# Splitting the first FFN weight behind its decode, with a power of two per row, mostly on GpSimd

## The chip, the core and the metric

The kernel runs on one NeuronCore of a Trainium2 chip. The core has five engines with instruction queues of their own, each of which runs its instructions in order: TensorE (PE in the profile; its weight loads are PEld), VectorE (DVE), ScalarE (ACT), GpSimd (POOL) and SyncE (SP, which here only issues DMAs). The metric is the device time of one execution in microseconds. The kernel before took 1120.02 us in the median of three runs (1115.86 to 1120.48).

## The reference

Causal attention with a forget-gate-like bias, followed by a two-layer FFN without an expert choice. Batch 8, 8 heads, 576 positions, head size 64; so x has 4608 rows of 512, the hidden layer has 2048. The two FFN weights arrive as float64.

```python
scores = scale * q @ k.T                      # scale = 1/8
cum = cumsum(maximum(s, 0))
scores = where(causal, -1e9, scores + minimum(-(cum_q - cum_k), 0))
attn = softmax(scores)
x = (attn @ v) as rows of 512                 # 8 heads side by side
h = x @ w_in                                  # 512 x 2048
g = where(h >= 1, h, where(h <= -1, 0, (h + 1)**2 / 4))
y = g @ w_out                                 # 2048 x 512
```

## The kernel before

**Products in two halves.** The FFN's products run in float16, but each operand is held as a high and a low half (`hi = f16(w * r)`, `lo = f16(w * r - hi)`), and three of the four half products are summed in PSUM. `r` is a power of two that brings the operand into float16's range. For the first weight (`w1`, `w_in`) there is one `r` for the whole weight before the change; for the second (`w2`, `w_out`) one for each half of its columns.

**The first weight.** `w_in` comes in 16 chunks of 128 x 512 numbers of 8 bytes (512 KB each): chunk c holds row block c // 4 of the weight (the 128 rows that are multiplied with head pair c // 4 of x) and column block c % 4. `Weights.load` issues a chunk's DMA; four raw buffers go round. `Weights.decode` turns a chunk from float64 into float32 in place in `WO[c]`: |w| on ACT (L203), the running peak (L204) and a shift (L205) on DVE, then for even chunks a byte shuffle on ACT (L210) and one DVE instruction (L211), for odd chunks two DVE instructions (L213, L214). When all 16 are decoded, `Weights.scale` forms the maximum over all peaks: a DVE reduction (L219), a transpose on PE (`row_wi`, L110), a few DVE instructions on one number, and a product with ones on PE that spreads it over the partitions (`col_wi`, L120). Then `Weights.split` writes the halves into `WI[c]`: hi on ACT (L232); lo on DVE in one instruction (L240) for eleven chunks, and for the five chunks of `POOL_LO` on GpSimd in two, a scaling in place (L235) and a subtraction (L238). The second weight goes the same way; its raw chunks use three buffers, and its first three loads are ordered behind the scale of the first weight (L190 copies that bound into the raw tile).

**Attention.** A job (n, hf) is a head pair n and a part hf of the query rows (hf 0: rows 0 to 319 in three tiles, hf 1: rows 320 to 575 in two). For each tile and head: scores on PE into PSUM (`s`, L409 for the first 12 jobs in plain float32, L412/L413 later), DVE adds the mask and finds the minimum (L418), ACT takes the exponential (L429). The first four jobs (`plain`, head pairs 0 to 3, hf 0) are done in float32: GpSimd scales the weights by the reciprocal sums (L446), PE transposes them into PSUM (`pp`, L450), ACT copies them (`pt`, L451), and PE multiplies with v (`px`, L502). Later jobs are split in halves and transposed by DMA (`pb`, `pt`, L476 to L483; `px`, L510). In all jobs px is then split into the two halves of x (L520 on ACT, L521 on DVE); the float32 jobs scale it by `exs`, a number of the batch.

**FFN.** For each batch b, part hf and block of 128 hidden columns (16 of them): `ffn_h` multiplies x with `WI` (12 matmuls, L562), ACT and DVE form the activation (L574, L577, L578), ACT and GpSimd split it (L588, L589), and `ffn_y` multiplies with `WO` (L601) into four PSUM banks `y0` to `y3`.

**Order.** The kernel is written as a list of steps: first the four float32 jobs with the decode of one first-weight chunk in every second slot, then the scale and the split of the first weight, then a loop in which attention slots, the decode and split of the second weight, and the FFN alternate. A scheduler with priorities then fixes every engine's order before the run; each engine follows its list in order, so an instruction whose input is late holds everything behind it on that engine.

The pieces of work that the change and the prediction touch are printed here.

Of the kernel before, what the change touches and what calls it, by code (L numbers as in the profile page):

```python
# [57 lines left out]
ACT_LOW = {'wi': range(0, 16, 2), 'wo': range(0, 16, 2)}  # L58
POOL_LO = {'wi': (2, 3, 7, 11, 15), 'wo': range(1, 16, 2)}
POOL_SCALE = ('wi',)  # L60
# [16 lines left out]
def attention_ffn(ctx: ExitStack, tc: tile.TileContext, qT, kT, vn, s, w_in, w_out, yT):  # L77
# [97 lines left out]
    class Weights:  # L175
        def __init__(self, name, src, held, out, tags, groups):
            self.size = NW // groups
# [3 lines left out]
            self.r = [cp.tile([P, 1], F32, name=f"r_{name}{g}") for g in range(groups)]  # L181
            self.raw = {}
            self.act_low, self.pool_lo = ACT_LOW[name], POOL_LO[name]

# [12 lines left out]
        def decode(self, c):  # L197
# [14 lines left out]
            else:  # L212
                V.scalar_tensor_tensor(wi, hw, -0x40000000, wi, ALU.bitwise_and, ALU.bitwise_or)  # L213
                V.scalar_tensor_tensor(wi, lw, 29, wi, ALU.logical_shift_right, ALU.bitwise_or)  # L214

        def scale(self, g, least):
            bound, r = self.bound[g], self.r[g]
            t = cp.tile([P, 1], F32, name=f"t_{self.name}{g}")
            V.tensor_reduce(t, self.peak[:, g * self.size:(g + 1) * self.size], axis=AX, op=ALU.max)  # L219
            top = column_max(t, f"{self.name}{g}")  # L220
            b = top.bitcast(I32)
            V.tensor_scalar(b, b, 3, -0x40000000, ALU.logical_shift_left, ALU.bitwise_xor)
            V.tensor_scalar(b, b, 0x7FFFFFFF, None, ALU.bitwise_and)
            pow2floor(top, top, least)
            spread(bound, top, f"{self.name}{g}")
            V.reciprocal(r, bound)
            V.tensor_scalar(r, r, 2.0 ** 14, None, ALU.mult)

        def split(self, c):
# [13 lines left out]
        "wi", lambda c: w_in[c // 4 * P:(c // 4 + 1) * P, c % 4 * NC:(c % 4 + 1) * NC, :],  # L243
        WO, WI, ((gp, "g", G_BUFS),), 1,
    )
# [17 lines left out]
    def batch_start(b):  # L263
        c = ap.tile([P, NPAIR], F32, tag="csc", name=f"c{b}")
        for p in range(NPAIR):
            v = vraw[b, p].rearrange("p j n -> p (j n)")
            V.tensor_reduce(c[:, p:p + 1], v, axis=AX, op=ALU.max, apply_absolute_value=True)  # L267
        t = ap.tile([P, 1], F32, tag="mt", name=f"mt{b}")
        V.tensor_reduce(t, c, axis=AX, op=ALU.max)
        top = column_max(t, f"m{b}")  # L270
        pow2floor(top, top, TINY)
        m = msc[b] = ap.tile([P, 1], F32, tag="mb", name=f"mb{b}")
        spread(m, top, f"m{b}")
        e = exs[b] = ap.tile([P, 1], F32, tag="ex", name=f"ex{b}")
        V.reciprocal(e, m)
        r = rcs[b] = ap.tile([P, 1], F32, tag="rcs", name=f"rc{b}")
        V.tensor_scalar(r, e, 4096.0, None, ALU.mult)

# [156 lines left out]
    def plain_t(n, i):  # L435
# [9 lines left out]
        for hd, Pt in enumerate(pbs.pop((n, i))):  # L445
            G.tensor_scalar(Pt[:R, :W], Pt[:R, :W], rs[:R, hd:hd + 1], 1.0, ALU.mult, ALU.mult)  # L446
            pp = ps_y.tile([P, 512], F32, tag=f"y{turn[0] % 4}", name=f"pp{n}_{i}_{hd}")
            turn[0] += 1
            for j in range(i + 1):
# [4 lines left out]
            )  # L454

    turn = [0]

# [32 lines left out]
    def att_out(n, hf):  # L490
# [3 lines left out]
        nj = tiles[-1] + 1  # L494
        PT, e = pts_.pop((n, hf)), 2.0 ** -12
        px = ps_s.tile([P, 512], F32, tag="s", name=f"px{n}_{hf}")
        if plain(n, hf):
            e = exs[b]
            for j in range(nj):
                lo = max(0, j * P - h_off)  # L500
                for hd in range(2):
# [3 lines left out]
                    )  # L505
        steps = [] if plain(n, hf) else [(j, vl, pl) for j in range(nj) for vl, pl in ((0, 0), (1, 0), (0, 1))]
        for m, (j, vl, pl) in enumerate(steps):
            lo = max(0, j * P - h_off)
            for hd in range(2):
                T.matmul(  # L510
                    px[hd * D:(hd + 1) * D, lo:N],
                    vts[n][:, vl, j, hd * D:(hd + 1) * D],
                    PT[:, 4 * j + 2 * hd + pl, lo:],
                    start=(m == 0), stop=(m == len(steps) - 1),
                )
        if p == 0:
            X[b, hf] = gp.tile([P, NKT, 2, N], F16, tag=f"x{hf}", bufs=2, name=f"x{b}_{hf}")
        x = X[b, hf]
        with tc.high_priority(offset=X_LEAD):
# [205 lines left out]
```

## Time and profile before

| | |
|---|---|
| times of three runs | 1115.86, 1120.02, 1120.48 us; median 1120.02 |
| profiled execution | 1121.97 us, of which the profile's span is 1120.2 us |
| busy share of the span | PE 91%, DVE 75%, PEld 69%, ACT 64%, POOL 60% |
| mean granted TensorE clock | 0.969 |
| instructions on GpSimd of the first weight's split (L235, L238) | 5 and 5 |

The profile's page gives the busy time of each engine, a picture of the span in 40 slices, and the costliest groups of instructions. Its timeline lists the instructions of one engine in order of time, merged where equal ones follow each other: start in us, duration in us, engine, line, operation, out<-in, sizes (partitions x elements) and count; in brackets how long the engine was idle before and whose result ended that. Its table by stretches gives the busy time of each engine between two moments, the granted TensorE clock, the share of the DMA engines' time and GB/s.

### The profile page before, as it was taken

How to read it: one execution, taken by the hardware profiler on the slowest of the kernel's cores; microseconds unless marked ns; L12 is line 12 of the kernel's file. 1: busy time of each engine (PE TensorE's matmuls, PEld its weight loads, DVE VectorE, ACT ScalarE, POOL GpSimd, SP SyncE). 2: the span in 40 equal slices, each digit the busy share in tenths (PEclk: the TensorE clock that was granted, in tenths of full speed). 3: DMA queues.
4: the chain of work that ended last, by engine and by line, in shares of the span. 5: the costliest groups of instructions: out<-in, count | busy, mean ns of one | idle time of the engine just before them, and what ended most of it. 6: DMA issues, size and time to landing. Idle time of an engine off the chain costs nothing. (4 is left out here: it accounts for less than half of the span.)

```text
span 1120.2 us, 24958 instructions
## 1 busy us (share of the span) xinstructions
PE 1018.8 (91%) x8494; PEld 777.5 (69%) x8494; DVE 844.7 (75%) x2364; ACT 716.5 (64%) x1695; POOL 676.0 (60%) x1149
## 2 busy tenths in 40 slices
PE   2584699899999999899999999999999999999998
PEld 1242366588777876687678877787678877787787
DVE  6759897678777877787778877887778877887533
ACT  3655586467557774777567764777477765777432
POOL 3446166676667665676567766666567666666522
PEclk9976799699999999999999999999999999999999
DMA  8823455546636763778548663667456762676300
GB/s 236 209 80 88 163 131 108 122 90 145 141 68 158 157 150 78 143 148 158 109 96 163 143 146 67 161 138 162 86 137 143 155 139 58 134 142 146 67 25 19
DMA packets 300839, 140.33 MB, mean 125 GB/s; under 512 B 237608, under 2 KB 286632, under 8 KB 300712
## 3 DMA queue, kind: packets, MB, share of 16 engines
q1 hardware_dynamic: 291008, 128.80, 53.5%
q10 hardware_dynamic: 9704, 9.93, 3.1%
q8 instruction: 67, 1.10, 0.4%
q14 instruction: 60, 0.49, 0.1%
HBM read 71.00 MB, written 9.73 MB: 72 GB/s over the span
## 5 line engine op out<-in xcount | busy, mean ns | idle before, releaser
L562 PE MATMUL h<-x,WI 128*128 128x256 f16 (+1 forms) x3072 | 456.8, 290 | 25.5 <-DVE u L578 20.4
L601 PE MATMUL y<-g,WO 128*128 128x256 f16 (+1 forms) x3072 | 450.9, 287 | 7.0 <-POOL g L589 4.8
L562 PEld LDWEIGHTS <-WI 128*128 128x128 f16 x3072 | 290.5, 99 | 120.5 <-issue 34.2
L601 PEld LDWEIGHTS <-WO 128*128 128x128 f16 x3072 | 288.7, 98 | 91.7 <-issue 12.5
L589 POOL TENSOR_TENSOR g<-u,g 128x320 f16<-128x320 f32 (+1 forms) x256 | 219.2, 856 | 200.6 <-ACT g L588 197.7
L429 ACT ACTIVATE p<-p,mn 64x64 f32<-64x64 f32 (+4 forms) x320 | 179.3, 560 | 135.3 <-DVE mn L418 119.0
L574 ACT ACTIVATE u<-h,ub,us 128x320 f32<-128x320 f32 (+1 forms) x256 | 149.3, 583 | 113.0 <-PE h L562 94.4
L577 DVE SCALAR_TENSOR_TENSOR h<-h,ws,u 128x320 f32<-128x320 f32 (+1 forms) x256 | 132.8, 519 | 94.4 <-ACT u L574 92.8
L418 DVE CUSTOM_DVE_ANT_0 p<-s,mask 64x64 f32<-64x64 f32 (+4 forms) x320 | 134.4, 422 | 55.8 <-PE s L413 39.0
L476 POOL TENSOR_SCALAR pb<-p,rs 128x256 f16<-128x256 f32 (+4 forms) x148 | 93.0, 629 | 134.0 <-DVE rs L472 47.9
L479 POOL TENSOR_TENSOR pb<-p,pb 128x256 f16<-128x256 f32 (+4 forms) x148 | 156.3, 1058 | 8.2
L482 DVE SCALAR_TENSOR_TENSOR pb<-p,rs,pb 128x256 f16<-128x256 f32 (+4 forms) x148 | 124.3, 840 | 20.6 <-POOL pb L476 20.4
L578 DVE SCALAR_TENSOR_TENSOR u<-u,r,h 128x320 f32<-128x320 f32 (+1 forms) x256 | 130.0, 508 | 5.2
L412 PE MATMUL s<-K1s,Q1s 128*128 128x288 f32 (+4 forms) x312 | 117.2, 378 | 10.6 <-DVE mn L418 6.7
L588 ACT CAST g<-u 128x320 f16<-128x320 f32 (+1 forms) x256 | 108.0, 422 | 22.4 <-DVE u L578 21.8
L477 ACT ACTIVATE p<-p,rs 128x192 f32<-128x192 f32 (+4 forms) x148 | 83.6, 569 | 54.9 <-DVE rs L472 54.5
L413 PE MATMUL s<-K2s,Q2s 68*128 68x288 f32 (+4 forms) x312 | 95.7, 308 | 0.1
L478 POOL TENSOR_SCALAR pb<-p 128x256 f16<-128x256 f32 (+4 forms) x148 | 92.6, 627 | 5.1 <-ACT p L477 2.5
L510 PEld LDWEIGHTS <-vt 128*64 128x64 f16 x1464 | 68.1, 112 | 19.5 <-issue 13.5
L510 PE MATMUL px<-pt,vt 128*64 128x256 f16 (+3 forms) x1464 | 77.2, 257 | 1.4 <-DMA pt<-pb 1.3
L412 PEld LDWEIGHTS s<-K1s,Q1s 128*128 128x128 f32 (+1 forms) x312 | 56.6, 182 | 22.7 <-DVE mn L418 3.8
L368 DVE TENSOR_TENSOR K2s<-rk,K1s 64x1152 fp32r<-64x1152 f32 (+1 forms) x52 | 59.2, 1139 | 7.5 <-ACT K1s L365 6.7
(131 smaller groups left out, 1013.3 us busy)
## 6 DMA issues: line engine op xcount, KB each, us to landing
rk<-in_k_dram SPq DMA_DIRECT2D x56, 288.0 KB
wir<-in_moe_w_in_dram SPq DMA_DIRECT2D x16, 512.0 KB
v<-in_v_dram SPq DMA_DIRECT2D x32, 256.0 KB
wor<-in_moe_w_out_dram SPq DMA_DIRECT2D x16, 512.0 KB
rk<-in_k_dram SPq DMA_DIRECT2D x48, 160.0 KB
rq<-in_q_dram SPq DMA_DIRECT2D x48, 160.0 KB
rq<-in_q_dram SPq DMA_DIRECT2D x56, 128.0 KB
out_dram<-o ACTq DMA_DIRECT2D x32, 160.0 KB
```

The costliest lines, as they stand in the source:

```text
L412: T.matmul(sc[:R, :c1 - c0], Q1[:, hd, qo:qo + R], K1[:, hd, c0:c1], start=True, stop=False)
L418: ttr[0] = V.tensor_tensor_reduce(out=Pt[:R, c0:c1], in0=sc[:R, :c1 - c0], in1=mask[:R, mo:mo + c1 - c0], scale=-0.125, scalar=3.0e38 if m ...
L429: A.activation(Pt[:R, :W], Pt[:R, :W], AF.Exp, bias=m2[:R], scale=-1.0, accum_out=sums[n, i][:R, hd:hd + 1])
L479: G.tensor_tensor(los[1], pw, his[1], ALU.subtract)
L482: V.scalar_tensor_tensor(los[0], pv, rs[:R, :1], his[0], ALU.mult, ALU.subtract)
L510: T.matmul(px[hd * D:(hd + 1) * D, lo:N], vts[n][:, vl, j, hd * D:(hd + 1) * D], PT[:, 4 * j + 2 * hd + pl, lo:], start=(m == 0), stop=(m ...
L562: T.matmul(h[:, :N], WI[4 * kt + ft // 4][:, wl, ft % 4 * P:(ft % 4 + 1) * P], x[:, kt, xl], start=(n == 0), stop=(n == 3 * NKT - 1),)
L574: first = A.activation(u, h[:, :N], AF.Relu, bias=ubi[b], scale=usc[b]).ins
L577: V.scalar_tensor_tensor(h[:, :N], h[:, :N], wsc[b], u, ALU.mult, ALU.max)
L578: V.scalar_tensor_tensor(u, u, r, h[:, :N], ALU.min, ALU.mult)
L589: G.tensor_tensor(g[:, 1], u, g[:, 0], ALU.subtract)
L601: T.matmul(ys[b, hf, m][:, :N], WO[8 * (m // 2) + ft // 2][:, wl, c0:c0 + P], g[:, gl], start=(ft == 0 and n == 0), stop=(ft == NFT - 1 an ...
```

## The change

Every block of 128 rows of the first weight now has a power of two of its own for each row (each partition), taken as soon as the block's four chunks are decoded (`row_scale`: five small DVE instructions, no transpose and no spreading). The chunks of a block are then split while the next block is decoded: in the code split(c - 4) follows decode(c), and the last four splits stand after the loop. Eleven chunks' lo halves go to GpSimd in two instructions, five stay on DVE; before it was five and eleven.

Because the rows of the weight now carry different powers of two, x has to carry the inverse share: `row_shares` forms the maximum over all rows (it still needs the transpose and the spreading on PE) and `shares`, a number per row, which scales x when it is split. The first four jobs' px therefore can't be split before the maximum is known: they are kept in PSUM, in the four banks of y, and split by `x_split` after the scale. The transposes pp, which used those four banks in turn, move to the two banks of h.

```diff
-POOL_LO = {'wi': (2, 3, 7, 11, 15), 'wo': range(1, 16, 2)}
+POOL_LO = {'wi': (0, 1, 2, 4, 5, 6, 8, 9, 10, 12, 14), 'wo': range(1, 16, 2)}
...
+        def exponent(self, b):
+            bi = b.bitcast(I32)
+            V.tensor_scalar(bi, bi, 3, -0x40000000, ALU.logical_shift_left, ALU.bitwise_xor)
+            V.tensor_scalar(bi, bi, 0x7F800000, None, ALU.bitwise_and)
...
+        def row_scale(self, k, least):
+            n = NW // NKT
+            b, r = self.rows[:, k:k + 1], self.r[k]
+            V.tensor_reduce(b, self.peak[:, k * n:(k + 1) * n], axis=AX, op=ALU.max)
+            self.exponent(b)
+            V.tensor_scalar(b, b, least, 2.0 ** -14, ALU.max, ALU.mult)
+            V.reciprocal(r, b)
+
+        def row_shares(self):
+            bound, e = self.bound[0], self.shares
+            t = cp.tile([P, 1], F32, name=f"t_{self.name}")
+            V.tensor_reduce(t, self.rows, axis=AX, op=ALU.max)
+            spread(t, column_max(t, self.name), self.name)
+            V.reciprocal(bound, t)
+            V.tensor_scalar(e, self.rows, bound, 2.0 ** -12, ALU.mult, ALU.mult)
+            V.tensor_scalar(bound, t, 2.0 ** 14, None, ALU.mult)
...
-            pp = ps_y.tile([P, 512], F32, tag=f"y{turn[0] % 4}", name=f"pp{n}_{i}_{hd}")
-            turn[0] += 1
+            pp = ps_h.tile([P, 512], F32, tag="h", name=f"pp{n}_{i}_{hd}")
...
         if plain(n, hf):
-            e = exs[b]
+            px = ps_y.tile([P, 512], F32, tag=f"y{p}", name=f"px{n}_{hf}")
...
+            held[n, hf] = px
+            return
...
+    def x_split(n, hf, px, shares):
...
-        x = X[b, hf]
+        x, e = X[b, hf], shares[:, p:p + 1]
         with tc.high_priority(offset=X_LEAD):
             A.activation(x[:, p, 0], px[:, :N], AF.Copy, scale=e)
             V.scalar_tensor_tensor(x[:, p, 1], px[:, :N], e, x[:, p, 0], ALU.mult, ALU.subtract)
...
                 w1.decode(c)
                 w1.load(c + 3)
+                if c >= NKT:
+                    w1.split(c - NKT)
+                if c % NKT == NKT - 1:
+                    w1.row_scale(c // NKT, LEAST_A)
...
     with tc.high_priority(offset=SCALE_LEAD):
-        w1.scale(0, LEAST_A)
+        w1.row_shares()
+        shares0 = cp.tile([P, NPAIR], F32, name="shares0")
+        V.tensor_scalar(shares0, w1.shares, rcs[0], None, ALU.mult)
         batch_scales(0)
+        for c in range(NW - NKT, NW):
+            w1.split(c)
     for c in range(3):
         w2.load(c, w1.bound[0])
-    for n in range(NW):
-        c = n % 4 * 4 + n // 4
-        w1.split(c)
     att_out(*jobs[NPAIR - 1])
+    for n, hf in jobs[:NPAIR]:
+        x_split(n, hf, held.pop((n, hf)), shares0)
```

The scheduler makes new lists of the written order. Three places matter for what follows. WO_126 to WO_141 are the first weight's 16 decoded chunks and WI_110 to WI_125 their split forms; r_wi_146 to r_wi_149 are the four row blocks' factors (before there is only r_wi_146); p_t_h is tile t and head h of the attention weights of the job at hand.

First, GpSimd at the end of the decode, where the third job's last tile (p_2) is scaled. Before:

```order
L404 MEMSET p_2_1_542 128x64
L404 MEMSET p_0_0_588 64x64
L446 TENSOR_SCALAR p_2_0_535<-p_2_0_535,rs_2_549 128x320
L446 TENSOR_SCALAR p_2_1_542<-p_2_1_542,rs_2_549 128x320
L377 TENSOR_SCALAR v_1_182<-v_1_182,rc_286 128x640
```

And in the changed kernel (L258 and L261 are the old L235 and L238, L468 is L446, L400 is L378):

```order
L258 TENSOR_SCALAR WO_138<-WO_138,r_wi_149 128x512
L426 MEMSET p_2_0_573 128x64
L426 MEMSET p_2_1_580 128x64
L258 TENSOR_SCALAR WO_140<-WO_140,r_wi_149 128x512
L400 TENSOR_TENSOR vt_943<-v_1_187,vt_943 128x640
L261 TENSOR_TENSOR WI_122<-WO_138,WI_122 128x512
L261 TENSOR_TENSOR WI_124<-WO_140,WI_124 128x512
L426 MEMSET p_0_0_630 64x64
L426 MEMSET p_0_1_637 64x64
L282 MEMSET v_1_1433 64x128
L468 TENSOR_SCALAR p_2_0_573<-p_2_0_573,rs_2_587 128x320
L468 TENSOR_SCALAR p_2_1_580<-p_2_1_580,rs_2_587 128x320
```

The split of two chunks of the last row block, which needs the last decoded chunk, and a product of v now stand ahead of the scaling that the third job's transposes wait for.

Second, DVE between the first weight's scale and its first instruction on the second weight (the peak of a decoded chunk, L204, in the change L207). Before:

```order
L240 SCALAR_TENSOR_TENSOR WI_123<-WO_139,r_wi_146,WI_123 128x512
L240 SCALAR_TENSOR_TENSOR WI_116<-WO_132,r_wi_146,WI_116 128x512
L297 TENSOR_SCALAR ws_722<-us_720 128x1
L240 SCALAR_TENSOR_TENSOR WI_120<-WO_136,r_wi_146,WI_120 128x512
L302 TENSOR_SCALAR gb_726<-gb_726 128x1
L240 SCALAR_TENSOR_TENSOR WI_124<-WO_140,r_wi_146,WI_124 128x512
L418 ISA p_4_0_919,mn_4_0_288_962<-s_4_0_288_960,mask,mn_4_0_0_923 128x288
L418 ISA mn_4_0_288_962 128x1
L521 SCALAR_TENSOR_TENSOR x_0_444<-px_0_775,ex_284,x_0_444 128x320
L471 TENSOR_SCALAR rs_3_905<-sm_3_855 128x2
L472 RECIPROCAL rs_3_905<-rs_3_905 128x2
L204 TENSOR_SCALAR WO_130,peak_wo<-WO_130 128x512
```

In the changed kernel:

```order
L549 SCALAR_TENSOR_TENSOR x_0_804<-px_0_736,shares_757,x_0_804 128x320
L312 TENSOR_SCALAR r_761<-r_761 128x1
L440 ISA p_3_1_925,mn_3_1_0_929<-s_3_1_0_927,mask 128x448
L440 ISA mn_3_1_0_929 128x1
L313 TENSOR_SCALAR r_761<-r_761 128x1
L314 TENSOR_SCALAR r_761<-r_761 128x1
L317 TENSOR_SCALAR us_769<-hs_759,r_761 128x1
L321 TENSOR_SCALAR ub_773<-r_761 128x1
L323 RECIPROCAL gb_775<-r_761 128x1
L319 TENSOR_SCALAR ws_771<-us_769 128x1
L324 TENSOR_SCALAR gb_775<-gb_775 128x1
```

The eleven L240 are gone from this stretch; three splits of x and the batch's small numbers remain, and two rows on scores and two on sums stand between the last row shown and the first L207.

Third, ACT behind the scale. Before, the sixteen hi halves stand between the last transposed copy and the first chunk of the second weight; the last four of them and what follows:

```order
L232 ACTIVATE WI_113<-WO_129,r_wi_146 128x512
L232 ACTIVATE WI_117<-WO_133,r_wi_146 128x512
L520 ACTIVATE x_0_444<-px_0_775,ex_284 128x320
L232 ACTIVATE WI_121<-WO_137,r_wi_146 128x512
L232 ACTIVATE WI_125<-WO_141,r_wi_146 128x512
L429 ACTIVATE p_3_0_856,sm_3_855<-p_3_0_856,mn_3_0_0_860 128x448
L429 ACTIVATE p_3_1_896,sm_3_855<-p_3_1_896,mn_3_1_0_900 128x448
L203 ACTIVATE WO_130<-wor_735 128x512
```

In the changed kernel:

```order
L548 ACTIVATE x_0_804<-px_0_462,shares_757 128x320
L548 ACTIVATE x_0_804<-px_0_602,shares_757 128x320
L548 ACTIVATE x_0_804<-px_0_736,shares_757 128x320
L451 ACTIVATE p_3_0_885,sm_3_884<-p_3_0_885,mn_3_0_0_889 128x448
L472 COPY pt_0_644<-pp_2_0_725 128x3x128
L472 COPY pt_0_644<-pp_2_1_731 128x3x128
L451 ACTIVATE p_3_1_925,sm_3_884<-p_3_1_925,mn_3_1_0_929 128x448
L206 ACTIVATE WO_128<-wor_788 128x512
```

The hi halves are gone from here (they stand among the decode's instructions, four after each block), and three splits of x are in their place.

More of the change, by code (lines that the diff above doesn't have):

```diff
@@ L175, in attention_ffn, with __init__ @@
     class Weights:
-        def __init__(self, name, src, held, out, tags, groups):
-            self.size = NW // groups
+        def __init__(self, name, src, held, out, tags, groups, by_rows=False):
+            self.size = NW // (NKT if by_rows else groups)
             self.name, self.src, self.held, self.out, self.tags = name, src, held, out, tags
@@ L180, in __init__ @@
             self.bound = [cp.tile([P, 1], F32, name=f"bound_{name}{g}") for g in range(groups)]
-            self.r = [cp.tile([P, 1], F32, name=f"r_{name}{g}") for g in range(groups)]
+            self.r = [cp.tile([P, 1], F32, name=f"r_{name}{g}") for g in range(NW // self.size)]
+            if by_rows:
+                self.rows = cp.tile([P, NKT], F32, name=f"rows_{name}")
+                self.shares = cp.tile([P, NKT], F32, name=f"shares_{name}")
             self.raw = {}
@@ L220, in scale @@
             top = column_max(t, f"{self.name}{g}")
[L221 to L224, printed above, removed]
+            self.exponent(top)
+            V.tensor_scalar(top, top, least, None, ALU.max)
             spread(bound, top, f"{self.name}{g}")
@@ L243, in attention_ffn @@
         "wi", lambda c: w_in[c // 4 * P:(c // 4 + 1) * P, c % 4 * NC:(c % 4 + 1) * NC, :],
-        WO, WI, ((gp, "g", G_BUFS),), 1,
+        WO, WI, ((gp, "g", G_BUFS),), 1, by_rows=True,
     )
@@ L273, in batch_start @@
         spread(m, top, f"m{b}")
-        e = exs[b] = ap.tile([P, 1], F32, tag="ex", name=f"ex{b}")
-        V.reciprocal(e, m)
         r = rcs[b] = ap.tile([P, 1], F32, tag="rcs", name=f"rc{b}")
-        V.tensor_scalar(r, e, 4096.0, None, ALU.mult)
+        V.reciprocal(r, m)
+        V.tensor_scalar(r, r, 4096.0, None, ALU.mult)
     def batch_scales(b):
@@ L454, in plain_t @@
             )
-    turn = [0]
     def weights_t(n, i):
@@ L494, in att_out @@
         nj = tiles[-1] + 1
-        PT, e = pts_.pop((n, hf)), 2.0 ** -12
-        px = ps_s.tile([P, 512], F32, tag="s", name=f"px{n}_{hf}")
+        PT = pts_.pop((n, hf))
         if plain(n, hf):
-            e = exs[b]
+            px = ps_y.tile([P, 512], F32, tag=f"y{p}", name=f"px{n}_{hf}")
             for j in range(nj):
@@ L505, in att_out @@
                     )
-        steps = [] if plain(n, hf) else [(j, vl, pl) for j in range(nj) for vl, pl in ((0, 0), (1, 0), (0, 1))]
+            held[n, hf] = px
+            return
+        px = ps_s.tile([P, 512], F32, tag="s", name=f"px{n}_{hf}")
+        steps = [(j, vl, pl) for j in range(nj) for vl, pl in ((0, 0), (1, 0), (0, 1))]
         for m, (j, vl, pl) in enumerate(steps):
@@ L515, in att_out @@
                 )
+        x_split(n, hf, px, w1.shares)
+    held = {}
+    def x_split(n, hf, px, shares):
+        b, p = n // NPAIR, n % NPAIR
+        N = HALF[hf][1]
         if p == 0:
             X[b, hf] = gp.tile([P, NKT, 2, N], F16, tag=f"x{hf}", bufs=2, name=f"x{b}_{hf}")
-        x = X[b, hf]
+        x, e = X[b, hf], shares[:, p:p + 1]
         with tc.high_priority(offset=X_LEAD):
```

## The prediction

> **What bounds the kernel now.** I read the table by stretches first, since an average over the span hides the start. Its columns are the stretch and its length, then busy time and count of PE, PEld, DVE, ACT and POOL, the granted TensorE clock, the DMA share and GB/s.
>
> ```profile
> 20.00:80.00 60.00, 39.73 (x132) 21.61 (x132) 39.16 (x154) 33.27 (x90) 25.73 (x61) 0.92 0.60 152
> 80.00:140.00 60.00, 34.00 (x147) 19.26 (x147) 52.41 (x116) 36.48 (x61) 24.19 (x26) 0.68 0.44 133
> 140.00:193.00 53.00, 50.07 (x365) 34.00 (x364) 45.21 (x111) 40.37 (x79) 37.89 (x46) 1.00 0.52 117
> 193.00:221.00 28.00, 22.00 (x128) 14.55 (x127) 19.94 (x80) 12.77 (x39) 17.31 (x37) 0.63 0.62 128
> 221.00:1060.00 839.00, 815.57 (x7242) 639.96 (x7241) 653.78 (x1839) 565.17 (x1373) 549.59 (x939) 1.00 0.61 128
> ```
>
> From 221 us on PE is busy 815.57 of 839 us at full clock: PE bounds the kernel there, and what it has done earlier it doesn't do again. The change can only move the start. In 80 to 140 us PE does 34.00 us in 60 and DVE 52.41: this stretch is DVE's. In 20 to 80 no engine is full; chains of short instructions set the pace. The second thing to read is therefore DVE's timeline behind the first weight's scale.
>
> ```profile
> 82.73 1.40 DVE L240 SCALAR_TENSOR_TENSOR WI<-WO,r_wi,WI 128x512 f16<-128x512 f32 x2
> 84.12 0.74 DVE L240 SCALAR_TENSOR_TENSOR WI<-WO,r_wi,WI 128x512 f16<-128x512 f32 x1
> 86.33 1.23 DVE L240 SCALAR_TENSOR_TENSOR WI<-WO,r_wi,WI 128x512 f16<-128x512 f32 x1
> 87.55 3.77 DVE L240 SCALAR_TENSOR_TENSOR WI<-WO,r_wi,WI 128x512 f16<-128x512 f32 x3
> 91.86 3.24 DVE L240 SCALAR_TENSOR_TENSOR WI<-WO,r_wi,WI 128x512 f16<-128x512 f32 x2
> 95.08 1.11 DVE L240 SCALAR_TENSOR_TENSOR WI<-WO,r_wi,WI 128x512 f16<-128x512 f32 x1
> 96.24 1.05 DVE L240 SCALAR_TENSOR_TENSOR WI<-WO,r_wi,WI 128x512 f16<-128x512 f32 x1
> 97.65 0.54 DVE L521 SCALAR_TENSOR_TENSOR x<-px,ex,x 128x320 f16<-128x320 f32 x1
> 98.38 0.67 DVE L204 TENSOR_SCALAR_CACHE_REDUCE WO<-WO 128x512 f32<-128x512 f32 x1
> ```
>
> The eleven lo halves take 1.40 + 0.74 + 1.23 + 3.77 + 3.24 + 1.11 + 1.05 = 12.5 us of the 15.7 between 82.73 and 98.38. Behind them wait the last part of x (97.65), without which PE can't finish a hidden block, and the first DVE instruction on the second weight (98.38). PE and the DMA queue show both waits:
>
> ```profile
> 75.33 0.37 PE L110 MATMUL row_wi<-ident,t_wi 128*1 128x128 f32 x1
> 81.90 2.18 PE L502 MATMUL px<-pt,v 128*64 128x320 f32 x10
> 98.24 1.23 PE L562 MATMUL h<-x,WI 128*128 128x320 f16 x4 [4.39 <-DVE x L521]
> ...
> 79.64 1.40 SPq L195 DMA_DIRECT2D wor<-in_moe_w_out_dram  x3
> 105.64 0.37 SPq L195 DMA_DIRECT2D wor<-in_moe_w_out_dram  x1
> ...
> 109.90 0.67 ACT L203 ACTIVATE WO<-wor 128x512 f32<-128x512 f32 x1 [3.33 <-DMA wor<-in_moe_w_out_dram]
> ```
>
> The first three loads of the second weight go out at 79.64, right behind the scale. The fourth goes out at 105.64 and ends an ACT wait at 109.90, so a load takes 4.26 us; the first would be usable at 83.9 and is first touched by DVE at 98.38.
>
> **What the change takes away here.** ACT loses sixteen hi halves, which begin in a row as soon as the scale is there:
>
> ```profile
> 79.71 8.68 ACT L232 ACTIVATE WI<-WO,r_wi 128x512 f16<-128x512 f32 x14 [0.38 <-DVE r_wi L227]
> 88.30 0.50 ACT L520 ACTIVATE x<-px,ex 128x320 f16<-128x320 f32 x1
> ```
>
> That is 0.62 us each. Without them and without DVE's 12.5 us the second weight's DVE work can begin one load and one |w| after the scale's DMA: 79.64 + 4.26 + 0.67 = 84.6 us, if the scale stays where it is. That is 98.4 - 84.6 = 13.8 us earlier. If the scale and the last float32 job come later by a slip S, the gain is 13.8 - S. The x chain says nearly the same: px ends at 84.08, its splits take 0.50 and 0.54, so PE's block could go on at 85.1 + S against 98.24, a gain of 13.1 - S. The three other splits of x, which now come after the scale too, are 1.5 us of ACT and 1.6 of DVE inside the 4.26 us in which the load is under way: nothing, and 1.5 us if the loads came at once.
>
> **What it puts ahead of it.** GpSimd's rows, and those of DVE at the end of the decode:
>
> ```profile
> 54.39 1.20 POOL L446 TENSOR_SCALAR p<-p,rs 128x320 f32<-128x320 f32 x2 [0.40 <-DVE rs L444]
> 60.74 2.25 POOL L446 TENSOR_SCALAR p<-p,rs 64x64 f32<-64x64 f32 x4 [3.08 <-DVE rs L444]
> 64.89 1.04 POOL L446 TENSOR_SCALAR p<-p,rs 128x320 f32<-128x320 f32 x2 [1.30 <-DVE rs L444]
> 67.54 1.40 POOL L378 TENSOR_TENSOR vt<-v,vt 128x640 f16<-128x640 f32 x1
> 87.37 0.75 POOL L235 TENSOR_SCALAR WO<-WO,r_wi 128x512 f32<-128x512 f32 x1
> 88.20 1.47 POOL L238 TENSOR_TENSOR WI<-WO,WI 128x512 f16<-128x512 f32 x1
> 89.65 2.22 POOL L235 TENSOR_SCALAR WO<-WO,r_wi 128x512 f32<-128x512 f32 x2
> 91.84 2.71 POOL L238 TENSOR_TENSOR WI<-WO,WI 128x512 f16<-128x512 f32 x2
> ...
> 52.44 1.68 DVE L214 SCALAR_TENSOR_TENSOR WO<-wir,WO 128x512 int32<-128x512 int32 x1
> 59.73 0.15 DVE L219 TENSOR_REDUCE t_wi<-peak_wi 128x1 f32<-128x16 f32 x1
> 61.19 0.72 DVE L214 SCALAR_TENSOR_TENSOR WO<-wir,WO 128x512 int32<-128x512 int32 x1
> ```
>
> A scaling of a chunk costs 0.75 to 1.11 us, a subtraction 1.36 to 1.47: 2.1 to 2.6 a chunk, 23 to 28 us for eleven, where GpSimd is busy 25.73 us of 60 now. By the sum they fit. By the order they don't quite. The third job's last tile is scaled at 64.89; in the new list two chunks of the last row block and a product of v stand ahead of it. They need the last decoded chunk (61.19 + 0.72 = 61.9), five small DVE instructions of 0.15 (62.7) and ACT's first hi half (63.3). Then GpSimd has 2 x 0.75 to 1.11, 1.40, and 2 x 1.36 to 1.47 to do: 5.6 to 6.5 us, so the tile is scaled at 68.9 to 69.8, 4.0 to 4.9 us late. PE's transposes of that job, its px and row_wi behind it, all in PE's order, are late by as much, and with them the scale.
>
> What of the third block's three chunks (6.3 to 7.7 us) comes on top? Their last chunk is decoded at 54.1 (the L214 of 52.44), so they can start at 55.5 and have 7.8 us, in which GpSimd also has the four scalings of 60.74 (2.25) and up to 1.2 us of the two of 54.39: 9.8 to 11.2 us of work, 2.0 to 3.4 too much. So S lies between 4.0 (all of the third block hidden) and 12.6 (4.9 + 7.7, none hidden). I take 4.5 + 3 = 7.5. Gain at the entry of the DVE stretch: 13.8 - 7.5 = 6.3 us, with bounds 1.2 and 9.8.
>
> Nothing else is on that path, as I read it. ACT's sixteen hi halves (9.9 us) go where it is busy 33.27 us of 60; DVE's five lo halves (3.5 at 0.70) and twenty small instructions (3.0) go where it is busy 39.16. Their cover is idle time between links of chains; without it the 16 us would push the decode, which the upper bound of S already allows for. The transposes' two banks in place of four make a pair wait at most for one copy of 0.5 us; px in the banks of y is gone by 95, long before y starts.
>
> **What reaches the end.** Two later places can swallow the gain.
>
> ```profile
> 109.78 18.79 SPq L195 DMA_DIRECT2D wor<-in_moe_w_out_dram  x7
> 134.30 0.18 PE L120 MATMUL col_wo<-t_wo,ones 1*128 1x1 bf16 x1 [4.62 <-DVE t_wo L118]
> 209.14 2.77 PE L510 MATMUL px<-pt,vt 128*64 128x256 f16 x30 [1.26 <-DMA pt<-pb]
> ```
>
> From 109.78 the second weight's loads go out one by one as raw buffers come free, and PE waits 4.62 us at 134.30 for a small number that stands behind them in DVE's list: this part follows the loads' pace more than its start. And in 193 to 221 PE has 22.00 us of work in 28 because attention is late (it waits for a transposed tile at 209.14): an FFN that arrives earlier waits longer for the same tile, unless attention comes earlier too. Bounds: all of the 6.3 or none. No row is nearer to one end, so I take half: 3.1 us. Against the profiled execution that is 1121.97 - 3.1 = 1118.9; this execution is 1.95 us above the median of the runs, so 1117 on the median's scale.
>
> **Rivals.**
>
> *GpSimd hides nearly all of it.* S is at its lower bound of 4.0 and the whole 9.8 us reaches the end, since DVE, which bounds 80 to 140, has 12.5 us less to do: 1120 - 9.8 = 1110. For it: GpSimd's 34 idle us. Against it: the order at 64.89.
>
> *GpSimd's queue becomes the path.* All of the attention weights of the first four jobs pass through GpSimd, in order, behind the split. If the added 23 to 28 us lie on the chain, S exceeds 13.8 and the sign turns; from S = 19.4 on it is slower by more than can be told from no change (0.5%, 5.6 us). At S = 22 it is 8 us: 1128; at 28, 1134. Against it: the jobs' chains also wait for PE, DVE and ACT.
>
> *The two engines get in each other's way.* These rows show one DVE instruction alone and a pair beside GpSimd's subtractions:
>
> ```profile
> 59.81 0.41 DVE L205 TENSOR_SCALAR WO<-WO 128x512 int32<-128x512 int32 x1
> 99.58 2.45 DVE L205 TENSOR_SCALAR WO<-WO 128x512 int32<-128x512 int32 x2
> 99.29 2.45 POOL L238 TENSOR_TENSOR WI<-WO,WI 128x512 f16<-128x512 f32 x2
> ```
>
> The pair takes 2.45 us, not 0.82, and L240 went from 0.70 to 1.26 and 1.62 in the same company. A decoded chunk has about 1.4 us of such DVE instructions (0.41, and 0.7 once or twice), twelve of them from 20 to 62 us: 17 of 42 us. Of 25 us added to GpSimd some 10 meet one; at half speed that is 5 us of DVE time on the decode. S becomes 12.5 and the gain 1.3: 1119, no change. The Trainium skill states this as a rule (GPSIMD Engine Reference, Key points: GpSimd shares its SBUF interfaces with VectorE, and contends with VectorE instructions in a two-port mode or with two SBUF inputs); the rows just shown agree with it, and it speaks against moving this work under the decode, where the kernel has most such instructions.
>
> **How the numbers follow.** Forecast (a gain of 0 to 5.5 us, middle 3): 0.40. First rival: 0.33. Queue on the path: 0.14. Contention: 0.13. Faster by over 0.5% is the first rival, 0.33; slower is the second, 0.14; within 0.5% are forecast and contention, 0.53. The range reaches from 1109, a microsecond below the first rival, to 1125, which leaves most of the second out; the forecast's own is 1114.5 to 1120.
>
> **What would show it.** Right: GpSimd's scaling of the third job's last tile, now at 64.89, between 69 and 77 us; row_wi, now at 75.33, some 7 us later; the second weight's first peak on DVE, now at 98.38, at 92 to 93; no L240 row behind the scale; the first y, which follows 134.30, 2 to 4 us earlier. Wrong: a first peak of the second weight behind 98, or row_wi behind 89, or a table by stretches in which 80 to 140 us gains but 221 us on is no shorter in sum with what lies before. Then the slip or the contention was mis-sized. A different pace from 221 us on would be outside this argument: the lists there are new too, and I have taken their pace as equal.

## The result, and the profile after

The changed kernel takes 1108.42 us in the median of four runs (1108.05 to 1110.02), the kernel before 1120.25 in the median of four beside it (1115.86 to 1121.04). The ratio is 0.9905, with a 95% interval of 0.9878 to 0.9933: faster, by 11.8 us as the medians have it and by 10.6 as the ratio has it (7.5 to 13.7). The median is 0.6 us below the range that was given, 1109 to 1125; the ratio on the 1120.02 us that the prediction started from gives 1109.4, its lower end. The likeliest case, no change that can be measured, did not come. The profiled execution took 1108.05 us (span 1106.3).

The table by stretches of the kernel after; columns as in the prediction:

```profile
80.00:140.00 60.00, 44.99 (x199) 25.39 (x199) 50.54 (x144) 37.25 (x70) 18.74 (x30) 0.76 0.52 156
...
221.00:1060.00 839.00, 822.45 (x7300) 648.50 (x7299) 674.46 (x1843) 571.28 (x1378) 531.55 (x941) 1.00 0.62 128
```

In 80 to 140 us PE now gets 44.99 us of work done in place of 34.00, with DVE at 50.54 in place of 52.41: the stretch that was looked at did change. The last row is the surprise. In the same 839 us PE was busy 815.57 us with 7242 matmuls before and 822.45 us with 7300 now. The prediction took the pace there as given. To compare many kernels I use one window, 270 to 1050 us, in which all run batches 1 to 7. The same table, of the kernel before, and then of the kernel after:

```profile
270.00:1050.00 780.00, 756.57 (x6700) 592.18 (x6698) 612.60 (x1728) 529.56 (x1283) 512.98 (x870) 1.00 0.62 130
```

```profile
270.00:1050.00 780.00, 763.45 (x6784) 600.64 (x6784) 631.66 (x1727) 535.08 (x1288) 495.49 (x873) 1.00 0.64 130
```

84 more matmuls in the same time, at 780 / 6700 = 0.116 us each, are 9.8 us: most of the 13.9 us by which the spans of these two executions differ (1120.2 and 1106.3). What PE waited for in that window shows where it comes from. The view of waits (line that waits, what it waited for: us in total, times, the longest) of the kernel before, then of the kernel after:

```profile
PE h L562 <- DVE u L578: 7.7, 9, 1.3
PE s L412 <- DVE mn L418: 6.7, 11, 1.3
PE y L601 <- POOL g L589: 4.8, 6, 0.8
PE s L412 <- DVE Q1s L367: 2.6, 7, 0.4
```

```profile
PE s L434 <- DVE Q1s L389: 5.2, 5, 1.2
PE s L434 <- DVE mn L440: 4.0, 6, 0.7
PE px L531 <- DMA pt<-pb: 2.5, 3, 1.1
PE h L590 <- ACT x L548: 2.2, 5, 0.4
```

The hidden block's wait for u (7.7 us) and y's wait for GpSimd (4.8) are gone; waits for Q1s and for a transposed tile take some of it back. Nothing in these batches was meant to be changed.

The start moved the way that the prediction's list of signs has it, but most of it came later than it said. DVE, GpSimd, PE and the DMA queue of the kernel after:

```profile
65.93 0.68 DVE L217 SCALAR_TENSOR_TENSOR WO<-wir,WO 128x512 int32<-128x512 int32 x1
...
77.54 1.61 POOL L468 TENSOR_SCALAR p<-p,rs 128x320 f32<-128x320 f32 x4
...
86.29 0.37 PE L110 MATMUL row_wi<-ident,t_wi 128*1 128x128 f32 x1
...
89.67 1.41 SPq L198 DMA_DIRECT2D wor<-in_moe_w_out_dram  x3
...
95.16 0.69 DVE L207 TENSOR_SCALAR_CACHE_REDUCE WO<-WO 128x512 f32<-128x512 f32 x1 [0.98 <-ACT WO L206]
...
138.59 0.45 PE L629 MATMUL y<-g,WO 128*128 128x320 f16 x2
```

The first y of the kernel before:

```profile
142.67 0.43 PE L601 MATMUL y<-g,WO 128*128 128x320 f16 x2
```

The third job's last tile is scaled at 77.54 (64.89 before, so 12.65 later). Of this, 4.7 us are there already when the last chunk is decoded (L217, the L214 of before): that ends at 66.61, before at 61.91. The other 8.0 us come between that decode and the scaling, which are 10.9 us apart now and were 3.0 before. row_wi comes at 86.29 (75.33), the second weight's loads at 89.67 (79.64, so 10.0 later), and its first peak all the same at 95.16 (98.38, so 3.2 earlier). The first y starts at 138.59, 4.1 us earlier than before.

### The profile page after: what moved, and what is told of

Same layout as the page of the kernel before. It is cut to its first block, busy times and chain, and to the rows that moved or that the text cites. A ratio compares the mean times of both kernels' runs of the same rounds, so it can differ in the third digit from the quotient of the medians.

```text
span 1106.3 us, 25041 instructions
## 1 busy us (share of the span) xinstructions
PE 1010.0 (91%) x8494; PEld 777.1 (70%) x8494; DVE 865.0 (78%) x2374; ACT 720.5 (65%) x1695; POOL 672.8 (61%) x1161
## 5 line engine op out<-in xcount | busy, mean ns | idle before, releaser
L590 PE MATMUL h<-x,WI 128*128 128x256 f16 (+1 forms) x3072 | 458.5, 289 | 18.4 <-DVE u L606 10.9
L629 PE MATMUL y<-g,WO 128*128 128x256 f16 (+1 forms) x3072 | 445.7, 287 | 3.6 <-DVE WO L263 1.5
L590 PEld LDWEIGHTS <-WI 128*128 128x128 f16 x3072 | 286.8, 99 | 110.3 <-issue 28.3
L617 POOL TENSOR_TENSOR g<-u,g 128x320 f16<-128x320 f32 (+1 forms) x256 | 208.8, 816 | 176.0 <-ACT g L616 168.0
L501 DVE SCALAR_TENSOR_TENSOR pb<-p,rs,pb 128x256 f16<-128x256 f32 (+4 forms) x148 | 127.8, 863 | 25.1 <-POOL pb L495 24.0
L497 POOL TENSOR_SCALAR pb<-p 128x256 f16<-128x256 f32 (+4 forms) x148 | 86.7, 586 | 23.8 <-ACT p L496 19.7
L390 DVE TENSOR_TENSOR K2s<-rk,K1s 64x1152 fp32r<-64x1152 f32 (+1 forms) x52 | 62.5, 1202 | 4.3 <-ACT K1s L387 3.2
```

The costliest lines, as they stand in the source:

```text
L501: V.scalar_tensor_tensor(los[0], pv, rs[:R, :1], his[0], ALU.mult, ALU.subtract)
L590: T.matmul(h[:, :N], WI[4 * kt + ft // 4][:, wl, ft % 4 * P:(ft % 4 + 1) * P], x[:, kt, xl], start=(n == 0), stop=(n == 3 * NKT - 1),)
L617: G.tensor_tensor(g[:, 1], u, g[:, 0], ALU.subtract)
L629: T.matmul(ys[b, hf, m][:, :N], WO[8 * (m // 2) + ft // 2][:, wl, c0:c0 + P], g[:, gl], start=(ft == 0 and n == 0), stop=(ft == NFT - 1 an ...
```

## First experiments: the place of the split, or the form of a scale

The change touches batches 1 to 7 in one instruction pair only: x is now split with a number per partition (`shares`) in place of the constant 2^-12. The planner, which fixes the order of every engine, gives another order as soon as that form is another. Theory 1: the gain is in these orders, and the place of the split has no part in it. Theory 2: the earlier start pays in every batch. Three kernels tell them apart.

*The kernel before, with x's factor in a tile* (`w1.share` is a 128x1 tile that holds 2^-12).

```diff
-        PT, e = pts_.pop((n, hf)), 2.0 ** -12
+        PT, e = pts_.pop((n, hf)), w1.share
```

> The kernel before with one change: from the fifth job on the splits of x take their factor of 2^-12 from a tile, one number per partition, as the changed kernel does, in place of a constant. The split of the first weight stays where it was. In the instruction lists this alone gives the order of the changed kernel for batches 2 to 5, on all four engines. Theory 1 (the lists): the pace from the first hidden block of batch 1 to the last one is a matter of this order, and the change of the split has no part in it. Then that block starts as before, at 267 us within 1, the way from it to the start of the last block takes 833.5 us as in the changed kernel and not 843.7, and the time is 1120.2 - 10.2 = 1110 us (1107 to 1113). Theory 2 (the start): the earlier FFN brings attention and FFN into a better phase, and this keeps paying in every batch. Then a longer split of x (0.49 against 0.40 us on ScalarE) gains nothing, the way takes 843.7 us, and the time is 1120 us (1118 to 1123).

Measured: 1108.93 us against 1119.35, ratio 0.9922 (0.9894 to 0.9950). This edit alone, with the split in its old place, gives 10.4 us, which cannot be told from the whole change's gain.

*The changed kernel, with the constant again* (`shares` is given for the first four jobs only).

```diff
-        x, e = X[b, hf], shares[:, p:p + 1]
+        x, e = X[b, hf], shares[:, p:p + 1] if shares is not None else 2.0 ** -12
```

> The changed kernel with one edit: from the fifth job on the splits of x take the constant 2^-12 again, so the row's share is left out for these jobs. The split of the first weight stays in its new place, and the lists of batches 2 to 5 are those of the kernel before. Theory 1 (the lists): the first hidden block of batch 1 starts at 263 us as in the changed kernel, the way from there takes 843.7 us as before, and the time is 1120.2 - 3.9 = 1116 us (1114 to 1118). Theory 2 (the start): 833.5 us for the way, and 1108.5 us in all.

Measured: 1119.14 us against 1119.35 over 12 and 17 runs, ratio 1.0002 (0.9983 to 1.0021). Everything that the change is named for, without the new form of the scale, is worth nothing that can be measured: 0.2 us faster by the medians, 0.2 slower by the ratio, with some 2 us of uncertainty either way. I had expected 1116: theory 1 was right on the pace, and its other half, 3.9 us from the start, did not come.

The two in the table by stretches, first the kernel before with the tile, then the changed kernel with the constant:

```profile
270.00:1050.00 780.00, 765.59 (x6785) 602.48 (x6784) 637.21 (x1739) 537.16 (x1293) 497.77 (x879) 1.00 0.64 132
```

```profile
270.00:1050.00 780.00, 757.10 (x6686) 592.22 (x6686) 616.47 (x1727) 529.85 (x1284) 511.33 (x872) 1.00 0.62 131
```

6785 matmuls with the tile (6784 in the changed kernel), 6686 with the constant (6700 in the kernel before). The pace follows the form of the scale and not the place of the split.

*The kernel before, with the tile on ScalarE alone.*

```diff
-            A.activation(x[:, p, 0], px[:, :N], AF.Copy, scale=e)
+            A.activation(x[:, p, 0], px[:, :N], AF.Copy, scale=e if plain(n, hf) else w1.share)
```

> The kernel before, where only ScalarE's half of the split of x takes its factor from a tile and VectorE's keeps the constant. This gives a third order in batches 2 to 5, unlike both others. Theory 1 (the lists): the first hidden block of batch 1 at 267 us, then a pace of its own: 833 to 850 us, and not that of the first run by necessity. A variant of theory 1, in which the longer instruction itself spaces the work and the order is by the way: 833.5 us as in the first run, 1110 us. Theory 2 (the start): 843.7 us, 1120 us.

Measured: 1107.02 us, ratio 0.9897 (0.9877 to 0.9917), 6822 matmuls in the window. A third order, and a gain again. With this run alone the variant could still stand that the longer instruction itself spaces the work.

## Is it the order? One wait taken away

The largest of the waits of before can be seen whole. In its timeline, DVE and PE around 552 us:

```profile
551.07 0.55 DVE L577 SCALAR_TENSOR_TENSOR h<-h,ws,u 128x320 f32<-128x320 f32 x1
551.53 0.50 DVE L418 CUSTOM_DVE_ANT_0 p<-s,mask,mn 128x288 f32<-128x288 f32 x1
...
551.97 2.98 DVE L267 TENSOR_REDUCE c<-v 128x1 f32<-128x640 f32 x4
554.88 0.53 DVE L578 SCALAR_TENSOR_TENSOR u<-u,r,h 128x320 f32<-128x320 f32 x1
...
555.46 1.79 PE L562 MATMUL h<-x,WI 128*128 128x320 f16 x12 [1.28 <-DVE u L578]
```

A hidden block's activation is the pair L577 and L578; only behind L578 is its PSUM bank free. Between the two stand the four reductions that form the next batch's maximum of v, 2.98 us in a row, and PE runs dry for 1.28 us. Every batch has this. In the kernel after the same four stand ahead of a pair, and PE has a block of y to do meanwhile:

```profile
547.06 2.99 DVE L290 TENSOR_REDUCE c<-v 128x1 f32<-128x640 f32 x4
549.97 0.54 DVE L605 SCALAR_TENSOR_TENSOR h<-h,ws,u 128x320 f32<-128x320 f32 x1
...
550.55 0.55 DVE L606 SCALAR_TENSOR_TENSOR u<-u,r,h 128x320 f32<-128x320 f32 x1
```

The next kernel is the one before, constant and all, where only these reductions are moved: `batch_max` is one of them, taken out of `batch_start`, which holds the rest.

```diff
-            if k == 5 and j + 1 < len(jobs) and jobs[j + 1][0] % NPAIR == 0 and jobs[j + 1][1] == 0:
+            if j + 1 < len(jobs) and jobs[j + 1][0] % NPAIR == 0 and jobs[j + 1][1] == 0 and k in (2, 3, 4, 5):
                 with tc.issue_after(ttr[0]):
-                    batch_start(jobs[j + 1][0] // NPAIR)
+                    for p in [i for i, m in enumerate((2, 3, 4, 5)) if m == k]:
+                        batch_max(jobs[j + 1][0] // NPAIR, p)
+                    if k == (2, 3, 4, 5)[-1]:
+                        batch_start(jobs[j + 1][0] // NPAIR)
```

> The kernel before, constant scale and old place of the split, with one thing moved on VectorE: the four reductions of the next batch's v (0.75 us each, 2.98 us in a row) are given out behind four pieces of the last job instead of all behind one. The instruction lists of TensorE are the same but for 0.3% of their entries. If waits by order in VectorE's list make the pace: the 1.02 to 1.28 us that TensorE waits once a batch for the u behind these reductions go (6.4 us over six batches), the way from the first hidden block of batch 1 to the start of the last block falls from 843.7 to 837 us and the time from 1119.4 to 1113 us (1111 to 1115). If order is only a by-product, and TensorE takes back elsewhere what a wait costs it: 843 us and 1119 us.

Measured: 1110.93 us against 1119.48, ratio 0.9918 (0.9888 to 0.9949). Its waits, in the same window:

```profile
PE s L420 <- DVE mn L426: 5.5, 10, 1.3
PE y L612 <- POOL g L600: 4.8, 6, 0.8
PE s L420 <- DVE Q1s L375: 2.7, 7, 0.4
PE h L573 <- DVE u L589: 1.3, 3, 0.4
```

The wait for u falls from 7.7 to 1.3 us, the others stay about as they were, and the time falls by 8.5 us (5.7 to 12.5 by the ratio) where 6.4 was expected from this wait alone. In its profile the way from the first hidden block of batch 1 to the start of the last block takes 836.5 us, where 837 was expected; it is 843.7 before and 833.6 in the kernel after. So order by itself, with every instruction as it was, moves the pace by 7 us where the change moved it by 10. That the longer split of x has no effect of its own is not shown by itself: each form of it that I built came with its own order.

The same edit with the slots 4 to 7 in place of 2 to 5, on top of the changed kernel with nine chunks on GpSimd (the next section tells why nine), is the best version I found:

```diff
-POOL_LO = {'wi': (0, 1, 2, 4, 5, 6, 8, 9, 10, 12, 14), 'wo': range(1, 16, 2)}
+POOL_LO = {'wi': (0, 1, 2, 4, 5, 6, 8, 9, 10), 'wo': range(1, 16, 2)}
...
-            if k == 5 and j + 1 < len(jobs) and jobs[j + 1][0] % NPAIR == 0 and jobs[j + 1][1] == 0:
+            if j + 1 < len(jobs) and jobs[j + 1][0] % NPAIR == 0 and jobs[j + 1][1] == 0 and k in (4, 5, 6, 7):
```

> The changed kernel with chunks 12 and 14 on VectorE as in the run before, and the four reductions of the next batch's v behind the last four pieces of the job instead of all behind one. It gives new lists from batch 1 on. If the pace is a matter of the order and this order keeps u ahead of the reductions: the waits for u, for the minima and for Q1s fall by 1 to 1.5 us a batch, and the time is 1104 - 8 = 1096 us (1094 to 1101). If the order in the changed kernel was about the best there is: 1104 us (1102 to 1107).

Measured: 1096.98 us, ratio 0.9801 (0.9775 to 0.9826) to the 1119.48 beside it; the change had 1108.42. Its row and its waits:

```profile
270.00:1050.00 780.00, 771.02 (x6858) 607.15 (x6857) 631.11 (x1732) 538.37 (x1291) 493.36 (x876) 1.00 0.63 130
...
PE y L640 <- POOL g L628: 3.5, 7, 0.8
PE px L539 <- DVE Q1s L397: 1.5, 1, 1.5
PE s L442 <- DVE mn L448: 1.4, 4, 0.4
PE h L601 <- DVE u L617: 0.9, 3, 0.3
```

PE is idle 9.0 of 780 us, where it was 23.4 before and 16.5 after the change.

## The start: GpSimd's share and the slip

*Two chunks of the last row block back to VectorE.*

```diff
-POOL_LO = {'wi': (0, 1, 2, 4, 5, 6, 8, 9, 10, 12, 14), 'wo': range(1, 16, 2)}
+POOL_LO = {'wi': (0, 1, 2, 4, 5, 6, 8, 9, 10), 'wo': range(1, 16, 2)}
```

> The changed kernel, with the two lo halves of the last row block that GpSimd has (chunks 12 and 14) given to VectorE. Nothing else differs, and the lists from batch 2 on are the same. If the slip of the start comes from GpSimd's order (two chunks of the last row block ahead of the third job's last tile): that tile, scaled at 77.54 us now, comes 4 to 5 us earlier, and with it the scale and the second weight's first peak, which ends at 95.9 now; VectorE has 1.4 us more to do, so the peak ends at 92 to 93.5, and the time is 1105.5 to 1108. If the slip is made by slower instructions all along (GpSimd and VectorE in each other's way) or by VectorE and ScalarE: the tile comes less than 2 us earlier, the peak ends at 95 to 97, and the time is 1108 to 1109.

Measured: 1104.20 us, ratio 0.9875 (0.9853 to 0.9897). Of its timelines:

```profile
63.22 0.68 DVE L217 SCALAR_TENSOR_TENSOR WO<-wir,WO 128x512 int32<-128x512 int32 x1
...
72.34 1.61 POOL L468 TENSOR_SCALAR p<-p,rs 128x320 f32<-128x320 f32 x4 [0.77 <-ACT p L451]
...
85.47 1.76 SPq L198 DMA_DIRECT2D wor<-in_moe_w_out_dram  x3
...
91.36 0.68 DVE L207 TENSOR_SCALAR_CACHE_REDUCE WO<-WO 128x512 f32<-128x512 f32 x1
```

The tile is scaled 5.2 us earlier, the loads go out 4.2 earlier, the first peak comes 3.8 earlier and ends at 92.04, as expected. Not all of this is the edit's. Up to the last row block the lists of VectorE and GpSimd are those of the kernel after, and this execution is 2.7 us ahead there already: its last chunk is decoded at 63.90, that of the kernel after at 66.61. From that decode to the scaling of the tile it is 8.4 us here and 10.9 there, so 2.5 us are the two chunks'. Other executions agree: 11.0 and 10.9 us in two other kernels with eleven chunks, 8.5 in the best version, with nine. So the slip from GpSimd's order, as the prediction described it, was there, and 2.5 of its 8.0 us go with two chunks. The time is 1.3 us below what I expected.

*Five chunks on GpSimd, and none.* `POOL_LO` is (2, 3, 7, 11, 15) in one and empty in the other; nothing else differs.

> The changed kernel with the lo halves divided as before: five chunks on GpSimd (2, 3, 7, 11, 15), eleven on VectorE, all in the new place behind their decode. If GpSimd's list is what makes the start late: the third job's last tile is scaled 5 us or more before 77.54 us, the second weight's first peak ends at 91 to 93, and the time is about that of the run with nine on GpSimd, 1103 to 1106 us. If VectorE's work under the decode is what counts (eleven halves at 0.7 are 7.7 us where it is busy 48 of 60 us): the peak ends at 96 to 99 and the time is 1108 us or more.

> The changed kernel with no lo half on GpSimd: all sixteen on VectorE, in the new place. It shows what of the slip is left when GpSimd has no part in the split. If the slip of 10 to 14 us is all GpSimd's: the third job's last tile is scaled at 66 to 68 us (64.89 before the change), the scale's loads go out at 81 to 83, and the second weight's first peak ends at 88 to 91. If VectorE then becomes the path (sixteen halves, 11.2 us, in its 12 idle us of 20 to 80): the tile comes at 70 to 74 and the peak at 92 to 95. The time is 1102 to 1107 us by the first, 1105 to 1109 by the second.

Measured: 1106.24 us with five (ratio 0.9882, 0.9853 to 0.9911), 1109.01 with none (0.9908, 0.9874 to 0.9943). With five the tile is scaled at 72.52 and the first peak ends at 92.36, as expected of GpSimd's list; the time is 0.2 us above its range. With none I was wrong by both theories: the tile comes at 76.67, almost as late as with eleven, and the first peak ends at 96.29. The rows of that kernel say why:

```profile
67.42 0.69 DVE L217 SCALAR_TENSOR_TENSOR WO<-wir,WO 128x512 int32<-128x512 int32 x1
...
72.31 0.74 DVE L263 SCALAR_TENSOR_TENSOR WI<-WO,r_wi,WI 128x512 f16<-128x512 f32 x1
73.11 3.08 DVE L263 SCALAR_TENSOR_TENSOR WI<-WO,r_wi,WI 128x512 f16<-128x512 f32 x3
76.10 0.17 DVE L465 TENSOR_SCALAR rs<-sm 128x2 f32<-128x2 f32 x1
...
76.67 1.61 POOL L468 TENSOR_SCALAR p<-p,rs 128x320 f32<-128x320 f32 x4 [2.02 <-DVE rs L465]
```

The last chunk is decoded at 68.11, later still than with eleven: VectorE now has the twelve halves of the first three blocks, 8.9 us, under the decode. And the last block's four halves stand ahead of the third job's reciprocal sums in VectorE's list, 3.8 us, as they stood ahead of its scaling in GpSimd's. Whichever of the two engines had these halves, they held the job, and with it the scale. An order that puts them behind the job was not tried.

## What the place of the split is worth

With the order the same in both, only the place differs in these two, and with it GpSimd's share, five chunks and eleven:

> The split in its old place, with the two edits that set the order: x's factor from a tile and the four reductions of v behind the last four pieces of the job. From batch 2 on its lists are those of the best version so far (but for DVE's reading of one name). It shows what the new place of the split is worth where the pace is the same. If nothing of the earlier start reaches the end: 1097 us (1096 to 1099) as the best version. If half of what is seen at the first y reaches it: the best version's first y came 6 us earlier than here, so 1100 us (1099 to 1102). If all of it does: 1103 us.

> The changed kernel as it is (eleven lo halves on GpSimd), with the four reductions of v behind the last four pieces of the job. The lists from batch 2 on are those of the run before this one and of the best version. If half of the start's gain reaches the end, with first y's that differ by 3 us from the one and 3 us from the other: between the two, 1098.5 us (1097 to 1100). If nothing reaches it: 1097 us for all three. If GpSimd's eleven halves cost as much as the new place saves: 1100 us, as the old place.

Measured: 1099.71 us with the old place (ratio 0.9824, 0.9796 to 0.9851), 1098.29 with the new one and eleven chunks on GpSimd (0.9803, 0.9776 to 0.9830), each as the half of the start's gain would have it, with intervals that do not exclude the other cases; and 1096.98 with nine. So there are three pairs with equal orders from batch 2 on. By the medians the new place with eleven chunks gains 0.2, 0.5 (1108.93 to 1108.42) and 1.4 us, by the ratios -0.2, 1.9 and 2.4, each within its uncertainty of some 2 to 3 us; with nine chunks it gains 4.7 (1108.93 to 1104.20) and 2.7 us by the medians. The second and the last of these five were not measured side by side.

The profiles of these kernels show the pace without the start. This is the way from the first hidden block of batch 1 to the start of the last block, in us, read off PE's timelines, with the kernel in brackets; the kernels of one row have the same order on all engines from batch 2 on:

| order | split in the old place | split in the new place |
|---|---|---|
| of the kernel before | 843.7 (before) | 842.4 (constant) |
| of the kernel after | 832.0 (tile) | 833.6 (after), 831.2 (nine), 832.3 (five), 833.8 (none) |
| with the reductions behind the last four pieces | 822.8 (tile) | 824.4 (eleven), 824.7 (nine) |

The order sets the pace, and the place of the split moves it by less than 2 us. The last two rows have the same form of the scale as well: between them order alone is worth 6.5 to 9.2 us.

Why does so little of the 4 us at the first y arrive? The prediction named the place. PE around 208 us in the kernel after:

```profile
207.95 2.77 PE L531 MATMUL px<-pt,vt 128*64 128x256 f16 x30 [3.35 <-DMA pt<-pb]
```

The tile that attention waits for came at 209.14 before, after 1.26 us of waiting; now it comes at 207.95 after 3.35: 1.2 us earlier, and the rest is waited away. The longer wait repeats; the earlier tile does not: the changed kernel with the constant, which has the same split, waits 3.37 us and gets the tile at 210.90, later than the kernel before. Single executions scatter by more than the gain: batch 1 starts at 263.9 to 269.6 us in the five profiles with the old place, and at 263.2 to 269.1 in the three with the new place and eleven chunks. From there to 221 us the execution of the kernel after gained again, but by the clock: the granted clock in 207 to 221 us is 0.83 here, and 0.50 in the kernel before and in the changed kernel with the constant:

```profile
207.00:221.00 14.00, 11.90 (x109) 9.48 (x110) 8.23 (x30) 7.51 (x23) 7.08 (x18) 0.83 0.59 126
```

```profile
207.00:221.00 14.00, 10.41 (x59) 7.04 (x59) 7.55 (x30) 6.87 (x22) 6.59 (x18) 0.50 0.65 129
```

The first row is of the kernel after, the second of the changed kernel with the constant.

## Why the prediction was right or wrong

- *"It bounds the kernel there, and what it has done earlier it doesn't do again. The change can only move the start."* This is the step that failed. PE bounds the stretch, but 23.4 of its 839 us were idle, in waits that came back in every batch at the same place, and the new order filled 7 of them. The prediction knew that the lists are new and took their pace as equal; in the two profiles the way from batch 1 to the last block fell from 843.7 to 833.6 us, 10 of the 13.9 us between them. It also had no term for the new form of x's scale, which sets those lists. Without that form the kernel takes 1119.14 us, inside the forecast's own 1114.5 to 1120.
- *Gain at the entry of 13.8 - S, with S taken as 7.5.* The form of the step was right, the size was off: the loads slipped by 10.0 us, within the bounds 4.0 and 12.6, the tile by 12.65, the upper bound, and the first peak came 3.2 us earlier in place of 6.3. What was missed is in "Nothing else is on that path": the last chunk is decoded 4.7 us late, and only the upper bound had room for that. Behind the decode the slip is 8.0 us, close to the 7.5 that was taken for all of it.
- *The signs of being right.* No L240 stands behind the scale. The others lie beyond what was given, the first and the last narrowly: the tile at 77.54 (69 to 77), row_wi 11.0 us later (some 7), the first peak at 95.16 (92 to 93), the first y 4.1 us earlier (2 to 4). None of the signs of being wrong came.
- *Half survives, 3.1 us.* The amount was too much, since only about half of the 6.3 us came at the entry. Half of the 3.2 that did come would be 1.6 us, and the three pairs, at 0.2, 0.5 and 1.4, leave that open; only the first excludes 3.1. The reason named for the lower bound, the late tile, is seen as a longer wait. The profile after alone would have misled: its blocks from 218 us on start 3.9 us earlier, which looks like this term and is partly the clock of one execution.
- *First rival, 1110.* Its time is near the measured one and its mechanism is not: S was 10.0 to 12.65 and not 4.0. The range reached down to 1109 for this rival's sake, so that the measured time lies at its end is luck.
- *Second rival, GpSimd's queue.* Half right: the queue did hold the third job, but S stayed below 13.8, and the sign did not turn.
- *Third rival, the two engines in each other's way.* Its mechanism is there. In 20 to 67 us the decode's 43 instructions on VectorE take 29.4 us, before 27.8, and those on the sums (L465, before L443) 3.7 in place of 1.6: 3.7 us more, where it had put 5. With no half on GpSimd these go back to 26.3 (42 instructions) and 1.6 us, but VectorE has the 8.9 us of halves in their place, so that kernel, as late as the one with eleven, doesn't clear it. How much of the decode's 4.7 us is due to it, and how much to the 2.4 us of halves and 2.6 of small instructions for the factors that VectorE got in the same stretch, stays open.

## What to carry to other kernels

Where a planner writes the order, any change of an instruction's form writes it anew everywhere, and a time of 1% may come from there; run the side effect alone (here one operand) and the change without it, before the gain is put down to the idea. An engine that is busy 97% of a stretch still has 3% that can be read: the waits that come back in each batch have one instruction in front of them, and moving four reductions apart was worth 8.5 us by itself, where the whole change was worth 11.8. Of work that is put under other work, look at the last piece: here it stood ahead of the very job that everything waits for, on both engines on which it was put.

## What was unexpected of the hardware

As I read these rows, GpSimd and VectorE kept each other out for several instructions in a row. In the kernel after, two scalings of 128x320 took 4.07 us at 57.66, and two like them 1.04 at 88.80; during the 4.07 us VectorE went through its own work:

```profile
57.66 4.07 POOL L468 TENSOR_SCALAR p<-p,rs 128x320 f32<-128x320 f32 x2
88.80 1.04 POOL L468 TENSOR_SCALAR p<-p,rs 128x320 f32<-128x320 f32 x2
73.42 1.38 POOL L400 TENSOR_TENSOR vt<-v,vt 128x640 f16<-128x640 f32 x1
74.77 2.25 POOL L261 TENSOR_TENSOR WI<-WO,WI 128x512 f16<-128x512 f32 x2
...
58.02 0.41 DVE L208 TENSOR_SCALAR WO<-WO 128x512 int32<-128x512 int32 x1
...
60.17 0.73 DVE L263 SCALAR_TENSOR_TENSOR WI<-WO,r_wi,WI 128x512 f16<-128x512 f32 x1
73.30 3.92 DVE L465 TENSOR_SCALAR rs<-sm 64x2 f32<-64x2 f32 x1 [0.47 <-ACT p L451]
80.97 0.17 DVE L465 TENSOR_SCALAR rs<-sm 128x2 f32<-128x2 f32 x1 [0.79 <-ACT p L451]
```

And the other way round: an instruction of two numbers per partition on VectorE took 3.92 us at 73.30, and 0.17 at 80.97; it ends when three subtractions of GpSimd, from 73.42 to 77.02, are through. The Trainium skill (SBUF — State Buffer, Who interferes with whom) says of VectorE's instructions in a two-port mode that whichever of the two engines issues first has the shared ports for its whole instruction, and that the other is blocked and not slowed. That it is blocked agrees with these rows, which do not show the mode; here it waited for three instructions. No run was made for this by itself.

A number per partition cost more than a constant here. The split of x on ScalarE, kernel before and kernel after:

```profile
L520 ACT ACTIVATE x<-px 128x256 f16<-128x256 f32 x26 | 9.7, 372 | 0.0
```

```profile
L548 ACT ACTIVATE x<-px,shares_wi 128x256 f16<-128x256 f32 x28 | 12.9, 461 | 3.8 <-PE px L531 3.8
```

89 ns more an instruction. The Trainium skill (ScalarE: Activation LUTs, What ACT_TABLE_LOAD costs) gives about 93 ns for each such operand, and the rows agree. The slower instruction went with the faster kernel.
